# K and V of the first batch in wider TensorE instructions: an attention and gated-FFN kernel

## The chip, the cores and the metric

The kernel runs on one core of a Trainium2 chip. The metric is the device time of one execution in microseconds (us); lower is better. The engines are TensorE (PE in the profile; PEld are its weight loads), VectorE (DVE), ScalarE (ACT), GpSimd (POOL) and SyncE (SP). A run of one core can't be told slow from fast by a neighbouring die; every timed comparison below uses runs that were marked fast, beside runs of the kernel before on the same chip. A "look" is the one execution of a run that the profiler took.

## The reference, cut to what matters

```python
k_proj = np.einsum('ks,bhsd->bhkd', E, k)        # E, F: 64 x 1024; k, v: 8 x 8 x 1024 x 64
v_proj = np.einsum('ks,bhsd->bhkd', F, v)
scores = scale * np.matmul(q, k_proj.transpose(0, 1, 3, 2))
attn = softmax(scores)                            # over 64 projected keys
x = np.matmul(attn, v_proj)                       # to 8192 x 512
out = (sigmoid(x @ w_gate) * (x @ w_val)) @ w_out # 512 -> 1536 -> 512
```

There are 8 batches. The attention of batch b + 1 is hidden among the FFN's matmuls of batch b. Only the first batch's attention has nothing to hide behind, and the change is about that.

## The kernel before

The start, cut. `busy` issues filler matmuls whose result nobody reads: they are meant to keep TensorE active, so that its clock comes up and stays up.

```python
EFT = sbuf("EFT", [P, NT, P], BF16)     # E (64 columns) and F (64 columns), transposed, 8 steps of S

def busy(n):                            # fillers of 128 columns
    for _ in range(n):
        mm(FB[3], bank[FB[3]][:, 0:P], ident[:, :], ident[:, :], ["ident"])

def project(n, w, bks, c0, R=None):     # w: 0 = E (K), 1 = F (V); R: heads 0-3 or 4-7
    width = 256 if R is None else 128
    for t in range(NT):
        for h in range(2):              # even heads in columns 0-63 of the array, odd in 64-127
            mm(bks[h], bank[bks[h]][64 * h : 64 * h + 64, c0 : c0 + width],
               EFT[:, t, 64 * w : 64 * w + 64], src[:, h, t, pairs(R), :], ...,
               start=(t == 0), stop=(t == NT - 1), tp=(0, 64 * h))

start_loads()          # SP: E, F; GpSimd: k heads 0-3, 4-7, q, q, v, v, then weights
constants()            # VectorE: identity, selection matrices
project_consts()       # 8 fp32 transposes of E and F, 2 evictions
busy(18)
...
k_part(0)              # project K of heads 0-3, evict 128x128 to kp
busy(4)
turn_k(whole, 0)       # 4 transposes of kp, evict to kpD
busy(10)
k_part(1)
busy(3)
qt(0, ("DVE", "ACT"))  # transposes of q, evictions on the engines named
turn_k(whole, 1)
sc(0)                  # scores and exp, heads 0-3
qt(1, ("DVE", "DVE"))
busy(6)
sc(1)
den(0)                 # sums of exp, then a reciprocal on VectorE
busy(4)
v_part(0)              # project V of heads 0-3; 2 evictions on ScalarE, 2 on VectorE
den(1)
keep = bc(0)           # broadcast of the reciprocals by matmul; evictions keep(0), keep(1)
...
xo(0)                  # eT by vpD, heads 0-3
keep = bc(1)
...
v_part(1)
```

Then the FFN starts; its first pair of steps has `xo(1)`, the product for heads 4 to 7, in its midst. Near 45 us the second half of the first batch is scaled by four multiplies in a row on VectorE (`bc2(0), bc2(1)`).

The softmax here doesn't subtract the row's maximum and nothing guards it: scores larger than these inputs give would overflow.

Of the kernel before, what the change touches and what calls it, by code (L numbers as in the profile page):

```python
# [8 lines left out]
BF16 = mybir.dt.bfloat16  # L9
# [109 lines left out]
def bass_linformer_attn__then__ffn_glu_sigmoid_kernel(  # L119
# [18 lines left out]
    with contextlib.ExitStack() as es:  # L138

        def sbuf(name, shape, dtype):  # L140
            return es.enter_context(nc.sbuf_tensor(name, shape, dtype))
# [13 lines left out]
        bsel8f = sbuf("bsel8f", [P, 4, 2, 64], FP32)  # L155

        EF = sbuf("EF", [P, S], FP32)
        EFT = sbuf("EFT", [P, NT, P], BF16)

        Qb = sbuf("Qb", [P, H, S // P * DH], BF16)  # L160
        KV = [sbuf(f"KV{i}", [P, H, S // P * DH], BF16) for i in range(3)]
# [30 lines left out]
        class Ring:  # L192
# [11 lines left out]
            (A0, A1, A2, A3, F0)  # L204
            + (A0, A1, F1, F2, A2)
            + (A3, F0, A0, A1, F1)
            + (A3, F0, A2)
            + (F2, A0, A1, F1)
            + (A3, A2, A0, A1, A3, A0)
        )  # L210
# [2 lines left out]
        def mm(b, o, lhsT, rhs, r, start=True, stop=True, tp=None, tr=False):  # L213
            kw = {}
            if tp is not None:
                kw["tile_position"] = tp
            if tr:
                kw["is_transpose"] = True
            else:
                kw["start"], kw["stop"] = start, stop  # L220
            return add("PE", lambda e: e.matmul(o, lhsT, rhs, **kw), r=r, x=[("bank", b)])  # L221
# [5 lines left out]
        def dve(fn, r, w, b=None):  # L227
            x = [] if b is None else [("bank", b)]
            return add("DVE", fn, r=r, w=w, x=x)
# [196 lines left out]
        def project_consts():  # L426
            ev = EF[:, :].rearrange("k (p t) -> k t p", t=NT)
            for g in range(2):
                b = whole.next()
                for t in range(4):  # L430
                    mm(
                        b,
                        bank[b][:, t * P : (t + 1) * P],
                        ev[:, 4 * g + t, :],
                        identf[:, :],
                        [("EF", "E"), ("EF", "F"), "identf"],
                        tr=True,
                    )
                act(
                    EFT[:, 4 * g : 4 * g + 4, :].rearrange("p t c -> p (t c)"),  # L440
                    bank[b][:, :],
                    [],
                    [("EFT", g)],
                    b=b,
                )


# [1 line left out]

        def busy(n):  # L450
            for _ in range(n):
                mm(FB[3], bank[FB[3]][:, 0:P], ident[:, :], ident[:, :], ["ident"])

        def pairs(R):
            return slice(0, NR) if R is None else slice(2 * R, 2 * R + 2)
# [20 lines left out]
        def keep_k(bk, c0, R=None):  # L476
            width = 256 if R is None else 128
            act(
                kp[:, pairs(R), :],
                bank[bk][:, c0 : c0 + width],  # L480
                [],
                [("kp", x) for x in both(R)],
                b=bk,
            )
# [38 lines left out]
        def VPD(R):  # L523
            return [("vpD", h, g, R) for h in range(2) for g in range(2)]

        def half_unit(hf, ring):
# [86 lines left out]
            def bc(R):  # L613
                bks = [ring.next(), ring.next()]
                for c in range(4):
                    for g in range(2):
                        n = 2 * R + g
                        nn = slice(32 * n, 32 * n + 32)
                        mm(
                            bks[g],  # L620
                            bank[bks[g]][:, c * P : (c + 1) * P],
                            (bsel8 if hf else bsel8f)[nn, c, :, :].rearrange("p h d -> p (h d)"),
                            (rhl if hf else rden)[nn, 0:P],
                            ["bsel8", ("rhl", R)] if hf else ["bsel8f", ("rden", 0, R)],
                            tp=(32 * n, 0),
                        )
                if hf:
                    for g in range(2):
                        scale(R, g, bank[bks[g]], xu[:, 2 * R + g, :], [("xu", 2 * R + g)], bks[g])

                def keep(g):
                    act(
                        rb[:, 2 * R + g, :],
                        bank[bks[g]][:, :],
                        [],
                        [("rb", 2 * R + g)],
                        b=bks[g],
                    )

                return keep  # L640
# [83 lines left out]
        def keep_kd(bk):  # L724
            act(
                kpd[:, :, :, :],
                bank[bk][0:64, :]
                .rearrange("p (h d) -> p h d", h=H)
                .unsqueeze(2)
                .to_broadcast([64, H, 2, DH]),  # L730
                [],
                ["kpd"],
                b=bk,
            )
            add(
                "SP",
                lambda e: e.dma_start_transpose(
                    kpD[:, :, :],
                    kpd[:, :, :, :].rearrange("p h g d -> p (h g d)"),
                ),  # L740
                r=["kpd"],
                w=[("kpD", 0), ("kpD", 1)],
                dma="kpD",
            )
# [357 lines left out]
        start_loads()  # L1102
        constants()
        project_consts()
        busy(18)
        qt, sc, den, bc, xo = half_unit(0, whole)

        def k_part(R):
            bk = whole.next()
            project(0, 0, [bk, bk], 0, R)  # L1110
            keep_k(bk, 0, R)

        def v_part(R):
            bks = [whole.next(), whole.next()]
            project(1, 1, bks, 0, R)
            keep_v(bks, 0, ["ACT", "DVE", "ACT", "DVE"], R)

        k_part(0)
        busy(4)
        turn_k(whole, 0)  # L1120
        busy(10)
        k_part(1)
        busy(3)
        qt(0, ("DVE", "ACT"))
        turn_k(whole, 1)
        sc(0)
        qt(1, ("DVE", "DVE"))
        busy(6)
        sc(1)
        den(0)  # L1130
        busy(4)
        v_part(0)
        den(1)
        keep = bc(0)
# [27 lines left out]
        for b in range(B):  # L1162
            todo = []
            for blk in (2 * b, 2 * b + 1):
                ms = [[m] for m in range(NF)]
                if blk <= 1:
                    ms = [[0, 1]] + ms[2:]
                if blk == 1:
                    gaps = {11: [0, 1, 2, 3]}
                else:  # L1170
                    gaps = {2: [0], 5: [1], 8: [2], 11: [3]}
                for m in ms:
                    if len(m) == 2:
                        todo.append(
                            lambda blk=blk: first_pair(blk, None if blk else lambda: xo(1))
                        )
                    else:
                        todo.append(lambda blk=blk, m=m[0]: mstep(blk, m))
                    if blk >= 1:
                        for tt in gaps.get(m[-1], ()):  # L1180
                            todo.append(lambda blk=blk, tt=tt: oproj(blk - 1, tt, ffn.next()))
            at = {}

            def put(i, fn):
                at.setdefault(i, []).append(fn)

            if b == 0:
                qt2, sc2, den2, bc2, xo2 = half_unit(1, att)
                put(4, lambda: (qt2(0, ("DVE", "ACT")), qt2(1, ("DVE", "ACT"))))
                put(5, lambda: (sc2(0), sc2(1)))  # L1190
                put(5, second_loads)
                put(7, lambda: (den2(), xo2(0), xo2(1)))
                put(9, lambda: (bc2(0), bc2(1)))
                spots = (12, 14, 15, 16, 17, 18, 19, 19, 20, 21, 23)
            elif b == 1:

                def kv2():
                    bk = att.next()
                    kv(2, bk)
                    keep_kd(bk)  # L1200
                    keep_vd(bk)

                put(3, kv2)
                spots = (8, 9, 11, 12, 17, 18, 19, 20, 20, 25, 27, 28, 30)
            else:
                spots = (3, 4, 6, 7, 12, 13, 14, 15, 15, 21, 23, 25, 27)
            if b + 1 < B:
                for i, fn in zip(spots, attention(b + 1)):
                    put(i, fn)

            def load_next(n):
                load_k(n)
                load_v(n)
                load_q(n)

            if b == 0:
                put(16, lambda: load_next(2))
                put(24, transpose_q)
            elif b + 2 < B:
                put(4 if b == 1 else 1, lambda b=b: load_next(b + 2))  # L1220
                put(20 if b == 1 else 16, transpose_q)
            for i, slot in enumerate(todo):
                slot()
                for fn in at.get(i, ()):
                    fn()
            assert max(at, default=0) < len(todo)
# [33 lines left out]
```

## Time and profile before

| | |
|---|---|
| time | 561.63 us median of 3 runs (561.59 to 562.26) |
| span of the profiled run | 559.7 us |
| TensorE busy | 550.6 us, 98% |
| first matmul; first K projection; first FFN matmul | 5.63; 9.28; 19.95 us |
| `xo(1)` starts | 20.93 us |
| from there to the end | 559.70 - 20.93 = 538.77 us |

How to read it: TensorE is busy 98% of the span, and from 24 us on it hardly waits. The first 20 us are different. They are a chain of small steps over three engines, with fillers in the gaps, and fillers count as busy too.

### The profile page before, as it was taken

The numbers are of one execution on the slowest core, as the hardware profiler recorded it, in microseconds if no ns is written. First come the engines' busy times: TensorE is split into PE (matmuls) and PEld (weight loads), VectorE is DVE, ScalarE is ACT, GpSimd is POOL, SyncE is SP. The second block draws the span as 40 slices with busy tenths as digits, with TensorE's granted clock in tenths as the row PEclk, the third lists the DMA queues.
The fourth block names the chain that finished last, engine by engine and source line by source line (L and its number), as shares of the span: only waits on it lengthen the run. The fifth ranks groups of instructions, "written<-read, shape, count | busy, mean of one in ns | idle before, by whom it ended". The sixth has DMA issues, their size and how long they took to land.

```text
span 559.7 us, 7742 instructions
## 1 busy us (share of the span) xinstructions
PE 550.6 (98%) x3057; PEld 249.4 (45%) x3057; DVE 257.0 (46%) x397; ACT 199.6 (36%) x358; POOL 113.2 (20%) x148
## 2 busy tenths in 40 slices
PE   5999999999999999999999999999999999999998
PEld 4544444444444444444444444444444444444444
DVE  4645363235733564344733456335553357433332
ACT  3563813533253422533226422345224422222220
POOL 9210201003700270004500063000900026000000
DMA  9999997924491359105591158802401101110012
GB/s 176 198 200 195 174 224 156 202 68 95 92 215 45 76 100 213 50 27 117 101 191 38 29 115 133 168 20 49 102 32 38 39 22 39 37 39 31 26 37 95
DMA packets 76564, 56.01 MB, mean 100 GB/s; under 512 B 34704, under 2 KB 68240, under 8 KB 76528
## 3 DMA queue, kind: packets, MB, share of 16 engines
q0 software_dynamic: 33984, 29.89, 34.5%
q1 hardware_dynamic: 42544, 25.63, 17.4%
q8 instruction: 24, 0.39, 0.3%
q14 instruction: 12, 0.10, 0.1%
HBM read 60.29 MB, written 16.78 MB: 138 GB/s over the span
## 4 chain that ended last, share of the span: by engine, by line
PE 98%; DMA 1%; DVE 1%; ACT 0%; issue 0%; SPq 0%
PE pF L221 92%; PE pA L221 6%; DMA EF<-in_F_dram 1%; DVE rden L596 0%; DVE xT L645 0%; DVE hT L1056 0%; ACT qT L225 0%; SPq L307 0%; DVE vpD L498 0%; DVE ost L1087 0%; ACT kp L225 0%
## 5 line engine op out<-in xcount | busy, mean ns | idle before, releaser
L225 ACT ACTIVATE sig<-pF 128x512 f32<-128x512 f32 x192 | 115.6, 602 | 297.2 <-PE pF L221 289.8
L1056 DVE SCALAR_TENSOR_TENSOR hT<-sig,pF 128x512 bf16<-128x512 f32 x192 | 131.6, 686 | 167.9 <-PE pF L221 129.4
L221 PE MATMUL pF<-xT,wV 128*128 128x512 bf16 x768 | 197.9, 379 | 0.3 <-DVE hT L1056 0.3
L221 PE MATMUL pF<-xT,wG 128*128 128x512 bf16 x768 | 198.0, 379 | 0.1
L221 PE MATMUL pF<-wO,hT 128*128 128x512 bf16 (+1 forms) x780 | 175.3, 376 | 0.0
L890 POOL PARTITION_BROADCAST rb<-rrow x96 | 76.9, 862 | 287.0 <-DMA rrow<-rden 281.9
L221 PEld LDWEIGHTS pF<-wO,hT 128*128 128x128 bf16 x780 | 75.3, 98 | 91.1 <-issue 2.5
L221 PEld LDWEIGHTS pF<-xT,wV 128*128 128x128 bf16 x768 | 75.0, 98 | 90.9 <-DVE hT L1056 1.0
L221 PEld LDWEIGHTS pF<-xT,wG 128*128 128x128 bf16 x768 | 73.0, 98 | 93.8 <-issue 7.1
L1087 DVE TENSOR_SCALAR ost<-pF 128x512 f32<-128x512 f32 (+1 forms) x65 | 44.4, 684 | 109.4 <-PE pF L221 109.4
L920 DVE TENSOR_TENSOR xT<-xu,rb 128x512 bf16<-128x512 f32 x48 | 39.2, 858 | 0.0
L816 DVE RECIPROCAL rden<-pA 128x128 f32<-128x128 f32 x26 | 24.6, 950 | 12.7 <-PE pA L221 12.7
L225 ACT ACTIVATE xu<-pA 128x512 f32<-128x512 f32 x46 | 24.5, 616 | 1.1 <-PE pA L221 1.1
L225 ACT ACTIVATE eT<-pF 128x512 bf16<-128x512 f32 x29 | 15.8, 595 | 22.9 <-PE pF L221 22.7
L225 ACT ACTIVATE eT<-pA 128x512 bf16<-128x512 f32 x35 | 19.3, 625 | 1.0 <-PE pA L221 1.0
L221 PE MATMUL pA<-KV,EFT 128*64 128x512 bf16 (+2 forms) x168 | 15.5, 323 | 0.0
L239 POOL DMA_DIRECT2D KV<-in_k_dram x9 | 8.0, 885 | 34.4 <-PE pF L221 34.4
L239 POOL DMA_DIRECT2D Qb<-in_q_dram x11 | 9.4, 865 | 14.7 <-PE pF L221 14.7
L221 PEld LDWEIGHTS pA<-KV,EFT 128*64 128x64 bf16 x168 | 8.0, 109 | 6.9 <-issue 2.9
L225 ACT ACTIVATE vpD<-pA 64x512 bf16<-64x512 f32 (+2 forms) x20 | 9.7, 485 | 1.0 <-PE pA L221 0.5
L225 ACT ACTIVATE xu<-pF 128x512 f32<-128x512 f32 x14 | 7.6, 594 | 3.7 <-PE pF L221 3.7
L221 PE MATMUL pA<-eT,vpD 64*64 64x512 bf16 (+1 forms) x112 | 8.4, 351 | 0.0
(78 smaller groups left out, 119.4 us busy)
## 6 DMA issues: line engine op xcount, KB each, us to landing
out_dram<-ost SPq DMA_DIRECT2D x63, 256.0 KB, 2.0
Qb<-in_q_dram POOLq DMA_DIRECT2D x7, 1024.0 KB, 19.8
KV<-in_k_dram POOLq DMA_DIRECT2D x7, 1024.0 KB, 9.8
KV<-in_v_dram POOLq DMA_DIRECT2D x7, 1024.0 KB, 14.9
wO<-in_moe_w_out_dram POOLq DMA_DIRECT2D x1, 1536.0 KB, 12.5
wG<-in_moe_w_gate_dram POOLq DMA_DIRECT2D x5, 256.0 KB, 17.7
wV<-in_moe_w_val_dram POOLq DMA_DIRECT2D x5, 256.0 KB, 18.3
KV<-in_k_dram POOLq DMA_DIRECT2D x2, 512.0 KB, 7.2
```

The costliest lines, as they stand in the source:

```text
L221: return add("PE", lambda e: e.matmul(o, lhsT, rhs, **kw), r=r, x=[("bank", b)])
L225: return add("ACT", lambda e: e.activation(o, i, func, scale=scale), r=r, w=w, x=x)
L239: add("POOL", lambda e: e.dma_start(o, i), r=r, w=w, dma=sem)
L816: lambda e: e.reciprocal(rden[:, cc], bank[bk][:, cc]),
L890: lambda e, n=n, i=2 * rnd + c, j=j, parts=parts: e.partition_broadcast(rb[0:parts, n, :], rrow[32 * j : 32 * j + 1, i, :], channels=parts),
L920: lambda e: e.tensor_tensor(xT[s][:, r, :, 256 * g : 256 * g + 256], xu[:, n, :].rearrange("p (f c) -> p f c", f=2), y.rearrange("p (f c) ...
L1056: lambda e: e.scalar_tensor_tensor(hT[blk % 2][:, m, :], sg[:, :], 1.0, bank[pv][:, :], ALU.add, ALU.mult,),
L1087: lambda e, pb=pb, c0=c0, c1=c1: e.tensor_scalar(o[:, c0:c1], bank[pb][:, 0 : c1 - c0], 0.5, None, op0=ALU.mult),
```

## The change

Its intent: fewer TensorE instructions while the first batch has the engine to itself. Four heads of K (both halves) and of V (heads 0 to 3) are projected by 8 matmuls of 256 columns in place of 16 of 128; fillers have 512 columns in place of 128, and there are fewer; K's turn takes its input with each head doubled, from 64 partitions; F is stored twice, so V's result comes out on all 128 partitions and needs one eviction (and one bank of results less, so one entry of the rotation of banks goes). Apart from that, the multiplies near 45 us are spread over two steps. Cut to its core:

```diff
-        EFT = sbuf("EFT", [P, NT, P], BF16)
+        EFT = sbuf("EFT", [P, NT, P + 64], BF16)      # F a second time, copied by VectorE
...
-                mm(FB[3], bank[FB[3]][:, 0:P], ident[:, :], ident[:, :], ["ident"])
+                mm(FB[3], bank[FB[3]][:, :], ident[:, :],
+                   ident[:, :].unsqueeze(1).to_broadcast([P, 4, P]), ["ident"])
...
-        busy(18)
+        busy(4)
...
+        def project_heads(n, bk, width, lhs, key, R):
+            for t in range(NT):
+                mm(bk, bank[bk][0:width, 0:256], EFT[:, t, lhs],
+                   KV[n][:, 4 * R : 4 * R + 4, t * DH : (t + 1) * DH], ..., tp=(0, 0))
         def k_part(R):
-            project(0, 0, [bk, bk], 0, R)
-            keep_k(bk, 0, R)
+            project_heads(0, bk, 64, slice(0, 64), "EFT", R)
+            act(kpd[:, 4 * R : 4 * R + 4, :, :], ...to_broadcast([64, 4, 2, DH]), ...)
...                                                   # k_turn: 4 transposes, [64 x 128] each
         def v_part(R):
+            if R == 0:
+                project_heads(1, bk, P, slice(64, P + 64), "FF", R)
+                act(vpD[:, 0:4, :]..., bank[bk][:, 0:256], [], VPD(R), b=bk)
+                return
...
         k_part(0)
-        busy(4)
-        turn_k(whole, 0)
-        busy(10)
+        k_turn(0)
+        busy(1)
         k_part(1)
-        busy(3)
         qt(0, ("DVE", "ACT"))
...
-        busy(6)
+        busy(1)
         sc(1)
         den(0)
-        busy(4)
+        busy(1)
...
-                put(9, lambda: (bc2(0), bc2(1)))
+                put(9, spread2)                       # matmuls of both, multiplies of bc2(0)
+                put(10, lambda: late[0]())            # multiplies of bc2(1)
```

More of the change, by code (lines that the diff above doesn't have):

```diff
@@ L206, in bass_linformer_attn__then__ffn_glu_sigmoid_kernel @@
             + (A3, F0, A0, A1, F1)
-            + (A3, F0, A2)
+            + (A3, A2)
             + (F2, A0, A1, F1)
@@ L439, in project_consts @@
                 act(
-                    EFT[:, 4 * g : 4 * g + 4, :].rearrange("p t c -> p (t c)"),
-                    bank[b][:, :],
+                    EFT[:, 4 * g : 4 * g + 4, 0:P],
+                    bank[b][:, :].rearrange("p (t c) -> p t c", c=P),
                     [],
@@ L445, in project_consts @@
                 )
+                dve(
+                    lambda e, g=g: e.tensor_copy(
+                        EFT[:, 4 * g : 4 * g + 4, P : P + 64], EFT[:, 4 * g : 4 * g + 4, 64:P]
+                    ),
+                    [("EFT", g)],
+                    [("FF", g)],
+                )
         def busy(n):
             for _ in range(n):
-                mm(FB[3], bank[FB[3]][:, 0:P], ident[:, :], ident[:, :], ["ident"])
+                mm(
+                    FB[3],
+                    bank[FB[3]][:, :],
+                    ident[:, :],
+                    ident[:, :].unsqueeze(1).to_broadcast([P, 4, P]),
+                    ["ident"],
+                )
         def pairs(R):
@@ L626, in bc, with scales @@
                         )
-                if hf:
+                def scales():
                     for g in range(2):
                         scale(R, g, bank[bks[g]], xu[:, 2 * R + g, :], [("xu", 2 * R + g)], bks[g])
+                if hf:
+                    return scales
                 def keep(g):
@@ L731, in keep_kd @@
                 [],
-                ["kpd"],
+                [("kpd", 0), ("kpd", 1)],
                 b=bk,
@@ L740, in keep_kd @@
                 ),
-                r=["kpd"],
+                r=[("kpd", 0), ("kpd", 1)],
                 w=[("kpD", 0), ("kpD", 1)],
@@ L1104, in bass_linformer_attn__then__ffn_glu_sigmoid_kernel, with k_turn @@
         project_consts()
-        busy(18)
+        busy(4)
         qt, sc, den, bc, xo = half_unit(0, whole)
+        def project_heads(n, bk, width, lhs, key, R):
+            for t in range(NT):
+                mm(
+                    bk,
+                    bank[bk][0:width, 0:256],
+                    EFT[:, t, lhs],
+                    KV[n][:, 4 * R : 4 * R + 4, t * DH : (t + 1) * DH],
+                    [("KV", n, R), (key, t // 4)],
+                    start=(t == 0),
+                    stop=(t == NT - 1),
+                    tp=(0, 0),
+                )
         def k_part(R):
             bk = whole.next()
-            project(0, 0, [bk, bk], 0, R)
-            keep_k(bk, 0, R)
-        def v_part(R):
+            project_heads(0, bk, 64, slice(0, 64), "EFT", R)
+            act(
+                kpd[:, 4 * R : 4 * R + 4, :, :],
+                bank[bk][0:64, 0:256]
+                .rearrange("p (h d) -> p h d", h=4)
+                .unsqueeze(2)
+                .to_broadcast([64, 4, 2, DH]),
+                [],
+                [("kpd", R)],
+                b=bk,
+            )
+        def k_turn(R):
+            bk = whole.next()
+            ob = bank[bk][:, :].bitcast(BF16)
+            for h in range(4):
+                mm(
+                    bk,
+                    ob[:, h * DH : (h + 1) * DH],
+                    kpd[:, 4 * R + h, :, :].rearrange("p g d -> p (g d)"),
+                    ident[0:64, 0:64],
+                    [("kpd", R), "ident"],
+                    tr=True,
+                    tp=(0, 0),
+                )
+            act(
+                kpD[:, 4 * R : 4 * R + 4, :].rearrange("p h c -> p (h c)"),
+                ob[:, 0:256],
+                [],
+                [("kpD", R)],
+                b=bk,
+            )
+        def v_part(R):
+            if R == 0:
+                bk = whole.next()
+                project_heads(1, bk, P, slice(64, P + 64), "FF", R)
+                act(
+                    vpD[:, 0:4, :].rearrange("p h d -> p (h d)"),
+                    bank[bk][:, 0:256],
+                    [],
+                    VPD(R),
+                    b=bk,
+                )
+                return
             bks = [whole.next(), whole.next()]
@@ L1118, in bass_linformer_attn__then__ffn_glu_sigmoid_kernel @@
         k_part(0)
-        busy(4)
-        turn_k(whole, 0)
-        busy(10)
+        k_turn(0)
+        busy(1)
         k_part(1)
-        busy(3)
         qt(0, ("DVE", "ACT"))
-        turn_k(whole, 1)
+        k_turn(1)
         sc(0)
         qt(1, ("DVE", "DVE"))
-        busy(6)
+        busy(1)
         sc(1)
         den(0)
-        busy(4)
+        busy(1)
         v_part(0)
@@ L1192, in bass_linformer_attn__then__ffn_glu_sigmoid_kernel, with spread2 @@
                 put(7, lambda: (den2(), xo2(0), xo2(1)))
-                put(9, lambda: (bc2(0), bc2(1)))
+                late = []
+                def spread2():
+                    first = bc2(0)
+                    late.append(bc2(1))
+                    first()
+                put(9, spread2)
+                put(10, lambda: late[0]())
                 spots = (12, 14, 15, 16, 17, 18, 19, 19, 20, 21, 23)
```

## The prediction

> **What bounds the kernel now.** I read the page first, then the chain that ended last in order of time, then the timeline of the first 25 us with the single starts of TensorE, then the landings of the first loads. The page says that TensorE is the bound almost everywhere:
>
> ```profile
> PE 550.6 (98%) x3057; PEld 249.4 (45%) x3057; DVE 257.0 (46%) x397; ACT 199.6 (36%) x358; POOL 113.2 (20%) x148
> PE 98%; DMA 1%; DVE 1%; ACT 0%; issue 0%; SPq 0%
> ```
>
> From 24 us on, the stretches show TensorE busy 21.00 of 21.00 us, later 510 of 512. The change does nothing there but in one place near 45 us. What it can move is the first batch's attention, 5.6 to 22.4 us, where "busy" is partly filler matmuls that compute nothing. So 98% says little here, and the chain must be read piece by piece:
>
> ```profile
> 5.63 1.95 PE pA L221 x8
> 7.57 1.78 PE pF L221 x18
> 9.35 0.70 PE pA L221 x16
> 10.05 0.02 issue
> 10.07 0.29 ACT kp L225
> 10.36 0.04 issue
> 10.40 0.30 PE pA L221 x4
> 10.71 1.51 PE pF L221 x29
> 12.21 0.46 PE pA L221 x8
> 12.67 0.02 issue
> 12.70 0.60 ACT qT L225
> ...
> 17.26 0.97 DVE rden L596
> ```
>
> The x18 are fillers; then come K's projection of four heads (16 matmuls), its eviction, its 4 transposes, then ten fillers, the second K (16) and three fillers in one piece, q's transposes and their eviction. This is a latency chain through TensorE, ScalarE and VectorE in turn; every link counts, and a filler counts only when it outlasts the wait that it fills.
>
> The loads are the other candidate. Issue plus time to landing in the trace gives K 7.6 and 10.3 us, q 11.6 and 12.9, V 15.5 and 19.1, the first gate weights 19.7. The uses start at 9.28 and 11.30, 12.05 and 13.58, 15.73 and 19.37, 19.95. So nothing waits for a load yet, but by only 0.2 to 0.3 us at V and the first weights. **A faster front could gain about 0.2 us at most before the loads bind; a slower one is not hidden.**
>
> [...] within one mode 128-column matmuls start 56 ns apart, at a change from filler to K projection 150 ns. So about 94 ns a change. [...] fillers start 107 ns apart until about 9.0 us, 56 ns after, though the page prints no granted clock. [...] The trace has 277 ns for 128, 384 for 256, 597 for 512, 1005 for 1024[...].
>
> **The change part by part.**
>
> *K's projection.* Before, 8 steps, each of two 128-column matmuls side by side in the two column halves of the array; V's show it best:
>
> ```profile
> 15.87 0.22 PE L221 MATMUL pA<-KV,EFT 128*64 128x128 bf16 x1
> 15.87 0.22 PE L221 MATMUL pF<-KV,EFT 128*64 128x128 bf16 x1
> 15.92 0.22 PE L221 MATMUL pA<-KV,EFT 128*64 128x128 bf16 x1
> 15.93 0.22 PE L221 MATMUL pF<-KV,EFT 128*64 128x128 bf16 x1
> ```
>
> A pair every 56 ns. After, 8 matmuls of 256 columns, nothing beside them: 2 x 53 + 3 = 109 ns each. So half as many instructions, but 8 x 109 = 0.87 us in place of 8 x 56 = 0.45. Start of the first to start of the last goes from 0.42 us to about 0.78, and the last streams 53 ns longer. The tiling removed the cost already; the instruction count was not what was paid for.
>
> *K's eviction.* Before 128x128, 277 ns:
>
> ```profile
> L225 ACT ACTIVATE kp<-pA 128x128 bf16<-128x128 f32 x1 | 0.3, 277 | 1.9 <-PE pA L221 1.9
> L225 ACT ACTIVATE kpd<-pA 64x1024 bf16<-64x1024 f32 x2 | 2.0, 1018 | 4.7 <-PE pA L221 4.7
> ```
>
> After, each head is written twice on 64 partitions: 512 elements a partition. Row two, its eight-head form in later batches, takes 1005 to 1018 ns; half the elements makes 597 by the other rows. Plus 0.32 us, twice, both on the chain. The turn stays at four transposes and a 128x256 eviction.
>
> *Fillers.* 18 of 128 at half clock, 1.92 us, become 4 of 512, 4 x 0.427 = 1.71, a little less as the clock comes up within the last: the first K projection starts at about 9.15 instead of 9.28. After the first turn, ten (0.66 us from first start to the next) become one (0.31 with the change of mode): minus 0.35. Three behind the second K go: minus 0.18. Four between K and its transposes only filled a wait. The later six, four and four become one each where the chain then waits for evictions anyway.
>
> *V of heads 0 to 3.* F is stored twice side by side, so the array is whole: 8 x 109 = 0.87 us against 0.57 from first start to next use[...]. Evictions: 2 ScalarE of 270 ns and 2 VectorE of 295 become one ScalarE of 384. This takes 0.62 us of VectorE away ahead of the second reciprocal, which before came up 0.39 us late: den's matmuls started at 16.30, and the first den shows 0.57 us from matmul to reciprocal, so 16.87, while the trace has 17.26.
>
> *Sum, by walking the chain with these gaps* (0.2 us plus streaming, and 0.1 more in a tiled mode, from the last matmul's start to its reader, as in the trace; 0.05 from eviction to matmul):
> K projection 9.15 to 9.93 (last start), eviction 10.36 to 10.95, transposes from 11.01 (before 10.40), filler 11.35, second K 11.66 (before 11.30), last start 12.44, q transposes 12.65 (before 12.05). The second K eviction, 12.87 to 13.46, now holds ScalarE when its half of q is ready at 13.30: q's eviction starts 13.36 and ends 13.96 (before 13.30). Second half of the scores 14.02 (before 13.35). The next scores' last part follows at 15.49 (before 14.83), den 15.72 (before 15.06), exp ends 16.98 (before 16.31), V 16.28, the second den 17.25 (before 16.30). There the freed VectorE gives back 0.4: reciprocal at 17.87 (before 17.26). The first broadcast, behind den, starts 17.64 (before 16.69), the second 19.07 (before 18.28). The FFN's first matmul then waits for xT from VectorE, which needs the broadcast's two evictions (19.32, 19.91) and two multiplies: **20.80, before 19.95**. The FFN runs without a gap from there, so the end moves by the same +0.85 us.
>
> *The spread multiplies near 45 us.* Today four multiplies of 0.62 us stand ahead of the last gate of block 0, and the first pair of block 1 waits for a bank:
>
> ```profile
> 43.19 2.48 DVE L645 TENSOR_TENSOR xT<-pA,xu 128x512 bf16<-128x512 f32 x4
> 45.58 0.68 DVE L1056 SCALAR_TENSOR_TENSOR hT<-sig,pF 128x512 bf16<-128x512 f32 x1
> 46.32 0.61 PE L221 MATMUL pF<-xT,wV 128*128 128x512 bf16 x2 [0.32 <-DVE hT L1056]
> ```
>
> TensorE loses 46.32 - (45.40 + 2 x 0.215) = 0.49 us. After, that gate goes in after two multiplies (44.70 to 45.39), the wait ends; but the other two finish at about 46.60, and the next matmuls, whose start was 46.76, need them: they start at about 46.65. The wait moves two steps on, and only 0.1 us is gained.
>
> Together +0.85 - 0.1 = +0.75 us on 561.63, so about 562.4; I lean slightly down, to 562.3, as the walk could be too pessimistic where waits overlap.
>
> **Rivals.** *A: it becomes faster.* Fewer instructions could matter if TensorE's sequencer or its instruction fetch were a limit. Against it: 128-column matmuls start 56 ns apart, 53 ns of which is streaming by the 512-column rows (215 ns); and every gap in the front is a wait for another engine, a change of mode or a filler. If the fillers cost more than I think, the loads allow about 0.2 us and the spread 0.1 to 0.5: 561.0 to 561.4. *B: the clock falls.* The fillers are there to hold the array's clock. After the change TensorE is idle about 0.95 us before the first turn and streams about 60% of 9.1 to 12.5 us. [...] For it: someone placed 45 fillers. Against: [...] the 512-column fillers stream as densely. I give it 1 in 10. *C: nothing changes,* because the front waits for loads. Against: each use now starts after its landing, so a delay isn't absorbed; only a gain is.
>
> **Range and chances.** The three runs before spread over 0.67 us. With that and an error of about half of the +0.75, the range is 561.4 to 563.1. Two per cent is 11.2 us, more than half the whole front of 16.8 us: the verdict is "same" almost surely; 0.985, with 0.005 for faster and 0.01 for slower.
>
> **What would show it.** In the profile after: K projections of 8 matmuls about 109 ns apart; the kpd eviction near 597 ns; the second K at about 11.7, the scores' second half at about 14.0, the reciprocal of the second half at about 17.9 with no V evictions on VectorE ahead of it; the first FFN matmul near 20.8; the wait near 45 us moved to the i = 2 matmuls and 0.4 us long; from 50 us on every interval as before. Wrong it would be if the first FFN matmul stands at 20.0 or earlier, if K's 256 columns stream faster than 109 ns, if the start of the warm clock moves by more than a few tenths, or if fillers start 107 ns apart per 128 columns after 9.1 us, which is rival B.

The sum: +0.85 us ahead of the FFN and -0.1 at the spread, together +0.75, so about 562.4. The gaps that the walk adds up are estimates from the first look of the kernel before, such as the 150 ns from the last filler to the K projection where fillers start 56 ns apart; a "mode" is the part of the array that a matmul uses, 128*128 or 128*64 in the timeline.

## The result, and the profile after

The changed kernel took 563.08 us (median of 4 runs, 562.73 to 564.12), the kernel before 561.69 beside it (4 runs, 561.59 to 562.26). The ratio is 1.0026 with a 95% interval of 1.0008 to 1.0043. A ratio here is the mean time of one kernel's fast runs over that of the other's of the same rounds, so it isn't quite the ratio of these medians. The loss is 1.39 us where I had forecast 0.75 by the walk.

The page of the changed kernel, its first part:

```profile
span 561.2 us, 7561 instructions
PE 547.4 (98%) x2940; PEld 248.1 (44%) x2995; DVE 257.4 (46%) x397; ACT 200.1 (36%) x357; POOL 113.2 (20%) x148
```

There are 62 weight loads fewer, 2995 after 3057, so the instructions are gone as intended. (The count of matmuls is lower still, since 55 of their records are missing from this trace.)

The chain that ended last in the changed kernel, in order of time (start in us, duration, what):

```profile
7.55 1.71 PE pF L221 x4
9.25 1.86 PE pA L221 x8
...
11.13 0.60 ACT kpd L225
```

The x8 after the four fillers is the first K projection: 1.86 us where the chain before has 0.70. The eviction takes the 0.60 that I had worked out. The timeline of TensorE, for the same kernel, has start, duration, engine, line, operation and shapes:

```profile
9.18 1.91 PE L221 MATMUL pA<-KV,EFT 128*64 128x256 bf16 x8
12.32 1.06 PE L221 MATMUL pF<-KV,EFT 128*64 128x256 bf16 x8
22.42 0.41 PE L221 MATMUL pA<-eT,vpD 64*64 64x256 bf16 x8
```

and for the kernel before:

```profile
9.28 0.64 PE L221 MATMUL pA<-KV,EFT 128*64 128x128 bf16 x16
11.30 0.64 PE L221 MATMUL pF<-KV,EFT 128*64 128x128 bf16 x16
20.93 0.41 PE L221 MATMUL pA<-eT,vpD 64*64 64x256 bf16 x8
```

The first two rows of the changed kernel are the same eight matmuls for two halves of the heads, and one takes nearly twice as long as the other. Their single starts are 213 ns apart in the first and 109 ns in the second. **The first K projection ran at half clock to its end** (in e5 below, 18 such matmuls stand in 3.80 us at a granted clock of 0.50, and 17 in 1.70 us at 1.00); I had it at full clock from 9.15. The fillers had ended, but the clock wasn't up. `xo(1)` comes 22.42 - 20.93 = 1.49 us later, and from there to the end is 561.18 - 22.42 = 538.76 us, against 538.77 before. So the whole loss lies ahead of `xo(1)`.

Near 45 us the changed kernel has

```profile
46.89 1.28 DVE L661 TENSOR_TENSOR xT<-pA,xu 128x512 bf16<-128x512 f32 x2
48.23 0.39 PE L221 MATMUL pF<-xT,wG 128*128 128x512 bf16 x1 [0.28 <-DVE xT L661]
```

The bank wait is gone, and the i = 2 matmul waits for the multiplies in its place, as forecast. From the broadcast's first matmul to this one it is 48.23 - 43.92 = 4.31 us, before 46.76 - 42.41 = 4.35: the spread gains 0.04 us on this stretch, not 0.1.

Two questions were left. Why did the clock come up later: did the change cause it? And what does the changed chain cost if the clock is up?

### The profile page after: what moved, and what is told of

Its sections match the earlier page's. It is cut to its first block, busy times and chain, and to the rows that moved or that the text cites. A ratio compares the mean times of both kernels' runs of the same rounds, so it can differ in the third digit from the quotient of the medians.

```text
span 561.2 us, 7561 instructions
## 1 busy us (share of the span) xinstructions
PE 547.4 (98%) x2940; PEld 248.1 (44%) x2995; DVE 257.4 (46%) x397; ACT 200.1 (36%) x357; POOL 113.2 (20%) x148
## 4 chain that ended last, share of the span: by engine, by line
PE 97%; issue 1%; DMA 1%; DVE 1%; ACT 0%; SPq 0%; DVEq 0%
PE pF L221 90%; PE pA L221 6%; DMA EF<-in_F_dram 1%; DVE ost L1103 0%; DVE xT L661 0%; ACT kpd L225 0%; DVE hT L1072 0%; SPq L307 0%; DVE qT L565 0%; DVEq L102 0%
## 5 line engine op out<-in xcount | busy, mean ns | idle before, releaser
L221 PE MATMUL pF<-xT,wG 128*128 128x512 bf16 x749 | 195.0, 379 | 2.3 <-issue 0.9
L221 PE MATMUL pF<-xT,wV 128*128 128x512 bf16 x751 | 195.4, 379 | 0.9
L221 PE MATMUL pF<-wO,hT 128*128 128x512 bf16 (+2 forms) x761 | 173.8, 376 | 1.3 <-issue 0.5
L221 PE MATMUL pA<-KV,EFT 128*64 128x512 bf16 (+3 forms) x160 | 17.2, 341 | 0.0
L221 PEld LDWEIGHTS pA<-KV,EFT 128*64 128x64 bf16 (+1 forms) x160 | 9.1, 112 | 8.0 <-issue 3.7
L225 ACT ACTIVATE vpD<-pA 64x512 bf16<-64x512 f32 (+3 forms) x19 | 9.6, 503 | 1.2 <-PE pA L221 0.7
L225 ACT ACTIVATE kpd<-pA 64x1024 bf16<-64x1024 f32 (+1 forms) x7 | 6.6, 949 | 7.6 <-PE pA L221 7.6
```

Of the source, the lines that this page charges most:

```text
L221: return add("PE", lambda e: e.matmul(o, lhsT, rhs, **kw), r=r, x=[("bank", b)])
L225: return add("ACT", lambda e: e.activation(o, i, func, scale=scale), r=r, w=w, x=x)
```

## The experiments

Three theories of the clock: **F**, wide fillers raise it later, as fewer instructions count for less activity; **T**, the long matmuls on half of the array hold it down; **W**, it rises at the end of a window that runs by itself, and the changed kernel met it at another point. I made 16 runs in four batches, each batch on one chip; three of them are the changed kernel unedited. All gave correct results.

### The fillers of the other kernel (e1, e2)

e1, the kernel before:

```diff
-        busy(18)
+        busyw(4)      # 4 fillers of 512 columns, as in the changed kernel
```

> The kernel before, with one edit: its first 18 fillers of 128 columns become 4 of 512; all else, the paired K projection too, stays. Theory F (the wide fillers raise the clock later, because there are fewer instructions or weight loads in the same stretch): TensorE is still at half clock in the first K projection, its pairs start 107 ns apart instead of 53, the full clock comes after 10.5 us, and the time is 0.4 to 0.9 us above before, about 562.3. Rival W (the moment the clock rises is set by a window that runs by itself, and the changed kernel was unlucky): [...] the times of the runs straddle those of before with no steady offset. Rival T (the long K matmuls on half of the array, not the fillers, hold the clock down): rise near 9.05 us, pairs 53 ns apart, time within 0.2 us of before.

e2, the changed kernel:

```diff
-        busy(4)
+        busyn(18)     # 18 fillers of 128 columns, as in the kernel before
```

> The changed kernel, with one edit: its first 4 fillers of 512 columns become 18 of 128 again; the later wide fillers stay. Theory F: full clock from about 9.05 us, the first K projection's 256-column matmuls 109 ns apart instead of 213, second K at about 11.7, first FFN matmul near 20.8, the time 0.6 us below the changed kernel, about 562.4. Rival W: rise at no fixed moment, times like the changed kernel's, 562.7 to 564.1. Rival T: the half clock in the K projection stays, 563.0.

Measured: e1 563.10 us (5 runs, 562.77 to 563.86), e2 563.16 (562.82 to 563.97), the kernel before on this chip 562.14 (11 runs, 561.48 to 563.15). In e1 the K pairs started 107 ns apart, as F expects, and the clock was up at about 10.9 us. But in e2, with its 18 narrow fillers back, the clock record rises at 10.75 us and half of the K projection ran 213 ns apart: F's forecast for e2 failed. There was a second surprise, in e1 here and in the next run: TensorE waited for K's load. So these two alone didn't decide, and the kernel before turned out to vary by 1.7 us on one chip.

### The spread alone (e3)

```diff
-                put(9, lambda: (bc2(0), bc2(1)))
+                put(9, spread2)
+                put(10, lambda: late[0]())
```

> The kernel before with only the multiplies near 45 us spread over two steps. My walk: the wait of 0.49 us for a bank goes, the i = 2 matmuls of the next pair then wait about 0.4 us for xT, gain 0.1 us, about 561.6. Rival: the gain is the whole 0.49 us, about 561.2. In the changed kernel's trace the interval from the first G of the pair to its i = 2 matmul is 2.19 us, before 2.23, which speaks for under 0.1.

Measured: 562.86 us (5 runs) beside 562.14; neither of the two numbers. From the broadcast to the i = 2 matmul it is 48.56 - 44.26 = 4.30 us, and from `xo(1)` to the end 561.50 - 22.75 = 538.75, 0.02 less than before. The spread is worth a few hundredths. The loss lies ahead of `xo(1)`, in code that e3 shares with the kernel before. Its timeline of TensorE:

```profile
9.88 0.64 PE L221 MATMUL pA<-KV,EFT 128*64 128x128 bf16 x16 [0.54 <-DMA KV<-in_k_dram]
12.47 0.64 PE L221 MATMUL pF<-KV,EFT 128*64 128x128 bf16 x16 [0.50 <-DMA KV<-in_k_dram]
```

In brackets stand the idle time and what ended it. The clock rose at 8.95 us here, so K's matmuls are fast, but the first K load landed at 9.83 us, not at 7.60 as in the first look, though it was issued at the same 1.34 us. The trace records the landing of a load as 16 shares, and the reader waits for the last. In the first look of the kernel before all 16 landed between 7.13 and 7.60; in e3 twelve had landed by 7.64, and the last four came at 8.09, 9.39, 9.71 and 9.83. The loads behind it come late too.

### K of the kernel before in the changed kernel (e4)

```diff
-            project_heads(0, bk, 64, slice(0, 64), "EFT", R)
-            act(kpd[:, 4 * R : 4 * R + 4, :, :], ...)
+            project(0, 0, [bk, bk], 0, R)
+            keep_k(bk, 0, R)                      # and turn_k in place of k_turn
```

> The changed kernel with K's projection, eviction and turn of the kernel before (16 paired matmuls, 128x128 eviction, four 128-column transposes); the wide fillers, V, and the spread stay. Theory F: the clock is still half in the first K projection (pairs 107 ns apart), so last pair at about 10.0, turn 10.7, second K 11.25; V in one eviction; about 562.0. Rival T: the clock rises at 9.05 as before, turn 10.3, about 561.6. Rival W: no fixed moment. If the K form alone costs what I worked out, this lies 0.6 to 1.3 us under the changed kernel.

Measured: the look spans 560.3 us, with `xo(1)` at 21.57; the rise falls in the midst of the K projection, at about 9.7. The six times fall into two groups, 561.97 to 562.61 and 564.55 to 565.28. The mean is 1.45 us above before, which no theory of mine explains, and no look fell into the upper group. The record has one hint: two of the three upper runs had a mean granted clock of 0.994, the lower three 0.999 or 1.0 (e7 and e8 below show what that means); the third upper run has 1.0. In the look itself q's transposes, V and the first gate matmuls wait for loads that land at 11.99, 15.82 and 20.56 us, so it can't show what K's form costs. This run is inconclusive.

### The clock by itself (e5)

```diff
+        for rep_ in range(6):
+            for kind, n in (("narrow", 72), ("wide", 18), ("half", 36), ("turn", 36)):
+                cool(2)          # two long ScalarE copies; the bout waits for them
+                fill(kind, n)    # 128 columns; 512; 256 on half of the array; fp32 transposes
+        cool(1)
         busy(18)
```

> A measurement of the clock by itself: the kernel before, with 24 bouts of TensorE work ahead of its fillers, each after about 10.6 us in which TensorE is idle (it waits for two long ScalarE copies into a weight buffer that is loaded later). Four kinds of bout, six of each: 72 fillers of 128 columns, 18 of 512, 36 matmuls of 256 columns on half of the array, 36 fp32 transposes. Read: how long after the bout's start the spacing halves. Theory F (the clock comes up later under wide fillers): narrow bouts rise after about 3.4 us or less, wide ones later, near 5 us or more, in every bout. Rival W (a window that runs by itself): narrow and wide rise at moments spread alike[...]. Rival T: half-array bouts rise later than narrow ones, or never. The time is some 400 us longer and says nothing.

The 3.4 us of theory F are those of the first look of the kernel before: its first matmul starts at 5.63 us, and the spacing of its fillers falls from 107 to about 60 ns at 9.07.

This is the run that decided. The stretches of e5 for a wide bout and for a narrow one, each before and after its rise (stretch, its length, busy time of PE, PEld, DVE, ACT and POOL with instruction counts, then the granted clock, DMA share, GB/s):

```profile
36.90:40.20 3.30, 3.23 (x8) 1.20 (x9) 0.00 (x0) 0.02 (x1) 0.00 (x0) 0.50 0.06 10
40.70:42.40 1.70, 1.70 (x9) 0.77 (x8) 0.00 (x0) 0.00 (x0) 0.00 (x0) 1.00 0.00 0
87.50:91.50 4.00, 3.97 (x38) 3.97 (x39) 0.00 (x0) 0.00 (x0) 0.00 (x0) 0.50 0.00 0
91.80:93.50 1.70, 1.70 (x33) 1.70 (x32) 0.00 (x0) 0.00 (x0) 0.00 (x0) 1.00 0.00 0
```

The granted clock is 0.50, then 1.00, for both. From the single starts I took the moment at which the spacing halves in each of the 24 bouts:

```
bout      start    rise after start   rise modulo 17.067 us
narrow    20.55    2.94               6.42
wide      36.97    3.39               6.22
half      53.63    4.05               6.47
turn      70.52    4.11               6.36
narrow    87.53    4.24               6.44
wide     104.57    4.24               6.41
half     121.56    4.27               6.36
turn     138.62    4.32               6.40
16 more            4.24 to 4.44       6.36 to 6.51
```

Whatever the kind of work, **all 24 rises fall at the same phase of a beat of 17.067 us**, within 0.29 us, less than one wide filler at half clock (0.43 us). The delay from the start of activity differs with where the start falls in that beat, from 2.94 to 4.44 us. The trace also holds the moments at which the granted clock changed, and they are sharper than the single starts: 23.53, 40.60, 57.66, 74.73 us and so on, each 17.067 us after the one before. The length comes from these moments; whether the beat is the whole 17.067 us or an equal part of it, they don't show.

One caution. Each bout starts a set time after the one before has ended, so the starts drift into step with the beat: from the fifth bout on they too are 16.99 to 17.10 us apart, and the clock record gives delays of 4.26 to 4.40 us, which a fixed delay would give as well. What speaks for a beat that runs by itself and against a fixed delay are the first four bouts, with 2.98, 3.62, 4.03 and 4.20 us by the clock record. The later twenty show that the kind of work doesn't matter, since all four kinds have the same delay there.

F and T fall: narrow, wide, half-array and even transposing bouts rise alike (from the fifth bout on all four kinds after 4.24 to 4.44 us by the single starts). W holds so far as these bouts show it: the rises kept a beat of 17.067 us, or an equal part of it, while the starts of the first four bouts were 16.42, 16.66 and 16.89 us apart. What sets the beat was not shown.

### The changed kernel again (e6)

No edit.

> The changed kernel, unchanged, once more, for a second look at its clock and loads and more times beside the kernel before on one chip. Theory W: the clock rises at another moment than in the first look (there after 10.9 us, as K ran at half clock to its end); times between 562.0 and 564.2; ratio to before 1.000 to 1.003. Theory F: half clock through the first K projection again, time 1.2 to 1.5 us above before.

Measured: 562.66 us (5 runs, 561.88 to 562.99); before, on this chip, 562.62 (9 runs, 561.83 to 563.19): ratio 1.0000, interval 0.9988 to 1.0013. The look's clock rises at 8.52 us, 2.80 after the first matmul, in the midst of the wide fillers:

```profile
8.94 1.06 PE L221 MATMUL pA<-KV,EFT 128*64 128x256 bf16 x8
21.32 0.41 PE L221 MATMUL pA<-eT,vpD 64*64 64x256 bf16 x8
```

The same eight matmuls, 1.06 us rather than 1.91, and `xo(1)` 1.10 us earlier than in the first look of this same kernel.

### Both kernels with the luck taken out (e7, e8)

In both, K is held back until the loads are in and the clock is up:

```diff
-        busy(18)      # busy(4) in the changed kernel
+        cool(1)       # two long ScalarE copies; the first K projection waits for them
+        cool(1)
+        for _ in range(150):
+            mm(FB[3], bank[FB[3]][:, 0:P], ident[:, :], ident[:, :], ["ident"])
```

> The kernel before with its first 18 fillers replaced by 150, and the first K projection held back until two long ScalarE copies are done (about 18.8 us), so that all early loads have landed and the clock is up. Together with the next run it takes both kinds of luck out. Expect: first K matmul to first FFN matmul 10.6 to 10.7 us as in the first look, time about 571.2, with a smaller spread than the kernel before shows.

> The changed kernel held back in the same way. My walk at full clock gives 11.65 us from the first K matmul to the first FFN matmul, against 10.67 before, so 0.98 us longer, less 0.1 at the spread multiplies: the time 0.8 to 0.9 us above the run before this one. If the walk is wrong and the half clock or the loads made the whole of the 1.4 us, the two settled kernels agree within 0.3 us. If the changed chain itself costs 1.4 us, the difference is 1.4 with full clock too.

The first K matmuls and `xo(1)` in the timeline of e7, held back like before,

```profile
19.06 0.64 PE L221 MATMUL pA<-KV,EFT 128*64 128x128 bf16 x16 [1.28 <-ACT wO L225]
30.68 0.41 PE L221 MATMUL pA<-eT,vpD 64*64 64x256 bf16 x8
```

and of e8:

```profile
18.73 1.03 PE L221 MATMUL pA<-KV,EFT 128*64 128x256 bf16 x8 [1.05 <-ACT wO L225]
31.08 0.41 PE L221 MATMUL pA<-eT,vpD 64*64 64x256 bf16 x8
```

From first K to `xo(1)` it is 11.62 us before and 12.35 after: **the changed chain is 0.73 us longer** with the clock up and nothing to wait for. The first look of the kernel before had 20.93 - 9.28 = 11.65 and e6 21.32 - 8.94 = 12.38, the same to 0.03. The times are 572.41 us (4 runs, 571.24 to 572.48) and 573.90 (5 runs, 571.67 to 575.04). They differ by more than the chains and still scatter, so the hold doesn't still the times; I rest on the intervals inside the traces.

The record shows why, in part. It lists the mean granted clock of every run; the stretch before the first recorded rise isn't counted in it (the first look of the changed kernel has 1.0). Both looks have 1.0. Their spans differ by 569.84 - 569.45 = 0.39 us, which with the 0.33 us that e8's K started earlier makes 0.72: the chain again. The other three runs of e7 have 0.997, the other four of e8 0.994. Over some 572 us that is half clock for about 3.4 and 6.9 us (my estimate: 0.003 and 0.006 of 572 us, doubled). So in those executions the clock fell again after it had come up; no look shows where.

### K alone and V alone, held back (e9, e10)

e9 is e7 with the new K part and turn only, e10 is e7 with the new V part and the second copy of F only; fillers and the rest are as before.

```diff
 # e9                                          # e10
-            project(0, 0, [bk, bk], 0, R)     -            bks = [whole.next(), whole.next()]
-            keep_k(bk, 0, R)                  -            project(1, 1, bks, 0, R)
+            project_heads(0, bk, 64, ...)     +            project_heads(1, bk, P, ..., "FF", R)
+            act(kpd[...], ...)                +            act(vpD[:, 0:4, :]..., ...)
```

> The settled kernel before (K held back to about 18.8 us, clock up, loads landed) with K's new projection, eviction and turn alone; its narrow fillers, V and the spread stay as before. Read from the trace: first K matmul to the first matmul of the second attention product (eT by vpD for heads 4 to 7), which is 11.62 us in the settled kernel before and 12.35 in the settled changed kernel. Theory K (K's form is what costs): 12.5 to 12.9 us, more than the whole change, since the fillers after the turn are not cut here. Rival V: under 12.0.

> The settled kernel before with V of heads 0 to 3 in 8 whole-array matmuls and one eviction alone (with the second copy of F). Same interval. By my walk the 8 matmuls take 0.3 us more ahead of den and the broadcast, VectorE gives 0.4 back at the second reciprocal but not at the first broadcast, so the interval is 11.8 to 12.0 us. Rival: the freed VectorE is what counts, interval under 11.6.

Measured, one look each, e9 first, then e10:

```profile
19.30 1.03 PE L221 MATMUL pA<-KV,EFT 128*64 128x256 bf16 x8 [1.79 <-ACT wO L225]
31.95 0.41 PE L221 MATMUL pA<-eT,vpD 64*64 64x256 bf16 x8
```

```profile
18.96 0.64 PE L221 MATMUL pA<-KV,EFT 128*64 128x128 bf16 x16 [1.15 <-ACT wO L225]
30.80 0.41 PE L221 MATMUL pA<-eT,vpD 64*64 64x256 bf16 x8
```

That is 12.65 us in e9, 1.03 more than e7, and 11.84 in e10, 0.22 more. Both fall in the forecast spans. K's form is what costs. The steps of e9 beside those of e7 show where: from the first matmul to K's eviction 1.07 us instead of 0.76, from there to the turn 0.65 instead of 0.34, and from the second K to q's transposes 1.17 instead of 0.75; the second eviction adds nothing. So 0.31 us of the 1.03 is the longer eviction, and the rest lies with the matmuls.

The whole change costs 0.73, so what remains, the cut in fillers, gives 1.03 + 0.22 - 0.73 = 0.52 us back. e8 beside e9 shows it directly: from the turn to the second K 0.54 us instead of 0.88, from the second K to q's transposes 1.00 instead of 1.17. I had 0.35 + 0.18 = 0.53 for these two places.

### The clock up before K in every run (e11, e12)

In both kernels:

```diff
+        dve(lambda e: e.memset(hT[0][:, 0, :], 0.0), [], [("hT", 0, 0)])
         constants()
+        for _ in range(40):
+            mm(FB[3], bank[FB[3]][:, 0:P], hT[0][:, 0, 0:P], hT[0][:, 0, 0:P], [("hT", 0, 0)])
         project_consts()
```

> The kernel before with 40 fillers of 128 columns on a zeroed buffer ahead of the transposes of E and F, from about 1.3 us, where TensorE idles until 5.6. Theory W[...] puts the rise[...] ahead of the first K projection in every run. The K projection then starts at its landing or near 8.3 us, not 9.28; from there the loads bind: gain 0.2 us in the lucky runs, up to 1 us in those where the clock came late; median 0.3 to 0.6 us under the kernel before. If the clock has no part in the spread, time and spread stay.

> The changed kernel with the same 40 early fillers. Its chain is 0.73 us longer at full clock, but K can start up to 1 us earlier, so the loads bind in part: median 0.0 to 0.5 us above the kernel before with early fillers, and 0.3 to 0.8 us below the changed kernel (562.7). If the clock was not the cause of the first look's 1.4 us, it stays at 562.7.

The clock did come up early, at 6.91 and 6.72 us in the looks. No time was gained: 563.19 us for e11 (6 runs), 563.44 for e12 (6 runs), 562.79 for the kernel before (11 runs); both intervals of the ratio include 1. Both forecasts of a gain failed. In the looks K's first load lands at 9.40 and 9.15 us and K, q and V wait for their loads, with `xo(1)` at 22.32 and 22.48: there the loads took all of the gain. The 0.16 us between the two isn't the cost of the chain, as e12's first load came 0.25 us earlier. In other runs the clock fell again: one of e11 and three of e12 have a mean granted clock of 0.997, and e12's three are its slowest (563.84 to 564.75, the others 562.42 to 563.04).

### More runs of the changed kernel, and a try at a faster one (e13 to e16)

e13 and e14 are the changed kernel once more. e15 is the kernel before with four small GpSimd memsets moved behind the issue of the K loads, e16 is e15 with e11's early fillers:

```diff
-            for i in range(4):
-                pool(... memset(quad ...))
             for R in range(2):
                 load_kv_heads(0, k, R)
+            for i in range(4):
+                pool(... memset(quad ...))
```

> The changed kernel once more, for its size beside the kernel before. Theory (chain 0.73 us longer when nothing else binds, less when loads come late; clock rise and landing vary from run to run alike in both): over the ten runs of this label and the next the mean lies 0.2 to 0.8 us above before. If the first comparison's 1.4 us is a property of the kernel: 1.1 to 1.7. If the second's: under 0.2. The look: rise anywhere from 8.4 to 12 us, first K load from 7.6 to 10.

> The same kernel again, as the run before: mean of both 0.2 to 0.8 us above before; clock and landing differ between the two looks by more than 0.3 us in at least one of them.

> The kernel before with the four small memsets of GpSimd behind the issue of the two K loads, which then starts at 0.72 instead of 1.34 us. Theory: all early loads land up to 0.5 us earlier; runs that wait for loads gain that, lucky ones gain nothing as their first K projection is held by fillers until 9.28: mean 0.1 to 0.5 us below before. Rival: the loads share the 16 engines with E and F, whose landing moves back by as much, and nothing is gained.

> Both: loads first, and 40 early fillers so that the clock is up ahead of K in every run. With neither the clock nor the issue in the way, 0.3 to 0.9 us below before, below both kernels. If the late engines set the landing whatever the issue, within 0.3 us of before.

Measured on one chip: before 562.43 us (11 runs, 561.33 to 563.36); e13 563.08 and e14 563.57 (6 runs each), ratios 1.0016 (0.9998 to 1.0034) and 1.0018 (1.0004 to 1.0033). The means of the twelve runs and of the eleven are 563.44 and 562.44: 1.0 us, a little over the 0.2 to 0.8 that I had written. In e13's look the first load landed at 8.24 and the clock record rises only at 11.61, 6.01 us after the first matmul; the first K projection ran at half clock to its end, 1.92 us from 9.18 on. In e14's the load came at 9.68, and the projection, 1.64 us from 9.73 on, began at half clock and ended at full.

e15 took 562.32 us (6 runs, ratio 0.9999) and e16 563.31 (5 runs, 1.0012): nothing gained, where I had forecast 0.1 to 0.5 and 0.3 to 0.9 us. In e15's look the K loads were issued at 1.23 us, only 0.11 earlier (the profile puts the 0.80 us of idle time before that down to GpSimd's queue), and the first landed at 7.81, no earlier than in the first look. In e16's look the clock was up at 4.89 us, but K, q and V waited for loads again. So no version here beats the kernel before.

e15 gave one thing unasked. Its clock rose after its K projection, so it shows what half clock costs the old form:

```profile
9.42 1.06 PE L221 MATMUL pA<-KV,EFT 128*64 128x128 bf16 x16
21.41 0.41 PE L221 MATMUL pA<-eT,vpD 64*64 64x256 bf16 x8
```

21.41 - 9.42 = 11.99 us, 0.37 over the 11.62 at full clock. For the changed kernel the first look has 22.42 - 9.18 = 13.24, 0.89 over its 12.35, and e13 has 13.24 again. The new form streams twice the columns one after another, so a late clock costs it more than twice as much.

## Why the prediction was right or wrong

**The bound, and where the loss would lie: right.** All of it stands ahead of `xo(1)`; the rest of the span is 538.76 against 538.77 us.

**The step that failed: "the first K projection starts at about 9.15", and "K projection 9.15 to 9.93 (last start)", at full clock.** The start was right (9.18), the clock wasn't. The last K matmul started at 10.68 and its eviction at 11.13, not 10.36. This term of the sum measured 0.89 us more than at full clock: 0.74 in the matmuls, and 0.14 between the last one's start and its eviction. With it the first look adds up: 0.73 for the chain + 0.89 for the clock - 0.10 for the earlier start of K = 1.52, measured 1.49 (these are the same intervals taken apart, so they must nearly close; the check is the 0.74 from the single starts). One of the prediction's own signs of being wrong was met: the start of the warm clock moved by more than a few tenths. I had read the one look of the kernel before ("until about 9.0 us") as a property of the work done, where in the probe the rises kept a beat of their own (17.067 us). In the looks with an unchanged opening the rise came from 2.80 us (e6) to 6.01 us (e13) after the first matmul, both in the changed kernel. That its opening has no part in this rests on these two and on the probe; the looks are too few to compare the openings of the two kernels.

**The walk at full clock: right in form, 0.25 us too long.** Without the spread it gave 11.65 us from the first K matmul to the first FFN matmul, 0.98 over before; the held-back pair differs by 0.73. Two terms were mis-sized: from the last 256-column matmul to its eviction I had 0.43 us, taken from paired matmuls, and e8 shows 19.80 - 19.49 = 0.31, twice; and the turn's matmuls, each with 64 moving columns, start 29 ns apart, not 56. The note that the longer eviction counts "twice, both on the chain" wasn't borne out either: in e8 q's eviction starts 0.65 us after q's transposes, as in e7, so the second one costs nothing.

**The parts: right.** K's form costs (1.03 us), V's a little (0.22), the fillers give back 0.52.

**The spread: right in mechanism, wrong in size:** 0.04 us on its stretch, not 0.1.

**Rival B (the clock falls), half met.** Its sign, half-clock spacing after 9.1 us, was there, but in no look of the two kernels did the clock fall during its work once it was up: it rose late, and it does so under narrow fillers too (e2, e15). The falls in e4, e7, e8, e11 and e12 were in runs without a look; the 21 runs of the changed kernel have a mean granted clock of 1.0, one of them 0.999. **Rival A (fewer instructions are faster): no sign of it. Rival C (the loads hide it): wrong in the first look, in part right in others,** where a first load that lands at 9.2 to 10 us sets the pace and hides part of the longer chain.

**The range was drawn from too little.** I took the scatter from three runs, 0.67 us, and the measured median lies at the very edge of the range. Over all batches the kernel before took 561.33 to 564.56 us in 46 runs. Against that, one comparison of four runs each says little: the three comparisons of the two unedited kernels gave 1.44 us (4 against 4 runs, means), -0.01 (5 against 9) and 1.00 (12 against 11). Weighted by the runs of the changed kernel that is some 0.8 us (an estimate). My 0.75 lies near it partly by luck, as the walk behind it was 0.25 us too long and the clock wasn't in it. The 1.39 is one draw from this scatter; the one run of its four that has a look had a late clock on top of the longer chain.

**Open:** why a few of the 16 shares of the first load land up to 2.4 us late in some runs; in which part of the run the clock fell in those with 0.994 and 0.997, and what else lifts e4's upper group; and how much of the scatter of times is clock and how much is loads, as a look shows one execution and most times have none.

## What to carry to other kernels

Count streamed columns, not instructions: two 128-column matmuls side by side in two halves of the array go by every 56 ns here, one matmul of 256 columns on one half every 109. Count the elements per partition of an eviction too: K's went from 128 to 512 (half the partitions, each head twice) and from 0.28 us to 0.59. What TensorE did in the first six microseconds of its activity could run at half clock (up to 6.01 us in e13), by chance and not by merit, so keep long streams off a critical chain there. Where the effect is smaller than the scatter, measure the interval inside the trace from one event to another with the luck held off, and compare the times only over many runs.
